# Letting the first chunks enter one a step in a convolution and token-mixing kernel

## The chip, the cores and the metric

The kernel runs on one core of one Trainium2 chip. Times are device microseconds of one execution of the whole program, and lower is better. TensorE (PE in the profile) multiplies, VectorE (DVE) and ScalarE (ACT) work on whole tiles, GpSimd (POOL) and SyncE (SP) mainly issue transfers.

## The reference

The first part is a causal depthwise convolution of seven taps over `x` of shape (8, 4224, 192), with eight heads of 24 channels whose taps are a softmax of `weight`. Its result is the `x` of the second part:

```python
theta = x @ w_theta
cos_t, sin_t = (np.cos(theta), np.sin(theta))
zr = x * cos_t
zi = x * sin_t
yr = np.einsum('ts,bsd->btd', w_tok_r, zr)
yi = np.einsum('ts,bsd->btd', w_tok_i, zi)
y = yr + yi
u = x + y
return (u + np.maximum(u @ w_ch, 0.0)).astype(np.float32)
```

The two token matrices are 4224 x 4224, so nearly all the work is two large matrix products over the tokens, with 8 x 192 = 1536 columns.

## The kernel before, in words

**Chunks and steps.** The 4224 input tokens are cut into 33 chunks of 128 (`NK`), the output tokens into 33 blocks of 128 (`NT`). Output blocks are taken in pairs, 16 pairs and one single block, which makes 17 units (`NU`). A step works on one unit: it multiplies the weights of that unit with every chunk that is active and adds the result to the unit's tile `pv` (128 x 1536 in float32). A chunk is active for 17 steps, so that it meets each unit once. `start[k]` is the step at which chunk `k` becomes active. At most eleven chunks (`NW`) are held at a time, so there are three rounds of eleven; chunk `k + 11` takes the place of chunk `k`. In a step `n` is the number of active chunks.

**Products.** For a pair of blocks the two matrices and two halves (cosine and sine) of a chunk are combined as in a fast 2 x 2 product: 7 products a chunk (a product is one weight tile times 768 columns, two matmuls of 384 columns). The products of a step come in seven runs, one for each combination, each over all `n` chunks; the single block has four runs (five if `n` is at most 2). In the first steps, while `n` is at most `NP`, a pair is multiplied plainly with eight products a chunk (`plain`). A run collects in a PSUM tile `y`, of which there are two buffers, and some runs go on collecting in the tile of an earlier one. After each run `give` adds `y` to a part of `pv` on VectorE (L461), or copies it there on ScalarE in the first round for the parts that are written first (L459).

**What a step needs.** The weights of a step are loaded on POOL's queue into `st` (`load_w`, L374, two steps ahead, one buffer for each of the two matrices), turned by VectorE in 32 x 32 blocks (`turn`, L387) and combined into the sums that the fast product needs (`wsum`, L399), one step ahead. `pv` of the step is loaded from a scratch `part` in device memory (`load_rows`, L425) unless this is the first round, and stored there again after the step (L549), unless it is the unit's last visit. The input `x` of the second part is added to `pv` once for each block: by POOL (`add_x`, L439, `adds`) after a load of the convolution's stored result `xs` into `xr`, or by an adding transfer (`add_ahead`, L448, `ahead`). In the unit's last visit the rest of the reference follows on `pv`: `cast`, a transpose, `output` (L585) and the store of the output.

**What a chunk needs.** A chunk's input `xw` is loaded by POOL's queue (L203) and the overlap with the previous chunk is copied on SP's queue (L194). `xw` and `pv` share six buffers. Its stages are two convolutions on PE (`conv`, L216) with evacuation (L156 or L154) and store to `xs` (L263); twelve transposes (L170) with one evacuation; two `theta` groups on PE (L146), each with two sines on ScalarE (L291); two products on VectorE (`product`, L297); and four differences on VectorE in two calls of `sums` (L306). The tile `z` of a chunk holds all seven operands of the fast product.

**Order.** The order of each engine's work is that in which the program writes it (`pe`, `dve`, `act` and `pool` chain each instruction to the one before); transfers without that wrapper are placed by the framework. Within a step `mix` writes the products and between them the events, which have a position in sevenths of the step. In the second and third round the stages of chunks that start in the next step are events of this step: `places` has two lists of positions, for a first and a second chunk. Chunks are loaded two steps ahead of their start.

In the first round the order is written out by hand at the end of the program: for `i` from 1 to 12, the stages of chunk `i` (convolution, transposes) and of chunk `i - 1` (theta, products, differences) are written with calls of `between` among them, and `between(n)` lets up to `n` products of the stream `flow` pass by `more(n)`, as long as they need no chunk above `ready`. That is at most eleven products for each `i`. After the loop the rest of the stream follows. `NPS` is the last plain step; chunks that started by then get their differences as events of the two steps from `NPS` on.

Of the kernel before, what the change touches and what calls it, by code (L numbers as in the profile page):

```python
# [16 lines left out]
def kernel(  # L17
# [34 lines left out]
    NK = S // P  # L52
# [7 lines left out]
    NU = (NT + 1) // 2  # L60
    NW = 11
    PC = 512
    NP = 4

    base = [0, 0, 1, 1, 2, 3, 3, 4, 4, 5, 5]
    assert len(base) == NW
    start = [base[k % NW] + (NU + 1) * (k // NW) for k in range(NK)]
    NSTEP = start[-1] + NU
    shift = (NU - 1 - (NSTEP - 1)) % NU

# [14 lines left out]
    def pe(ins):  # L85
        return in_order("pe", ins)
# [96 lines left out]
    class Chunk:  # L183


        def __init__(self, k, before=None):
            self.k = k
            self.xw = wk.tile([2 * WR, 2, B, D], F16, name="xw", tag="big", bufs=6)
            for a in range(NQ):
                h, lo = a // 2, (a % 2) * WR  # L190
                t0 = token(k, a)
                hist = self.xw[lo : lo + HALO, h, :, :]
                if before is not None:
                    nc.sync.dma_start(  # L194
                        out=hist, in_=before.xw[lo + Q : lo + Q + HALO, h, :, :]
                    )
                elif t0 == 0:
                    nc.vector.memset(hist, 0.0)
                else:
                    lo, t0 = lo - HALO, t0 - HALO  # L200
                lo += HALO
                n = (a % 2 + 1) * WR - lo
                nc.gpsimd.dma_start(  # L203
                    out=self.xw[lo : lo + n, h, :, :],
                    in_=x[:, t0 : t0 + n, :].rearrange("b s d -> s b d"),
                )
# [117 lines left out]
    def load_chunk(k):  # L324
        if k < NK and k not in chunks:
            chunks[k] = Chunk(k, before=chunks[k - 1] if k % NW else None)

    def active(t):
        return [k for k in range(NK) if start[k] <= t < start[k] + NU]

    def unit(t):
        return (t + shift) % NU

    class Step:


        def __init__(self, t):
            self.t, self.u, self.ks = t, unit(t), active(t)
            self.n = len(self.ks)
            self.tbs = [tb for tb in (2 * self.u, 2 * self.u + 1) if tb < NT]  # L340
            self.pair = len(self.tbs) == 2
            self.first = t < NU
            self.final = t + NU >= NSTEP
            self.late = self.final and self.n < NW
            visits = [v for v in range(NU, NSTEP) if v % NU == t % NU]
            quiet = [v for v in visits if start[2 * NW - 1] < v <= 2 * NU]
            self.adds, self.ahead = [], []
            for i, tb in enumerate(self.tbs):
                known = self.known(tb)
                if t not in ([v for v in quiet if known < v - 1] or visits[-1:])[:1]:  # L350
                    continue
                if not self.late:
                    self.adds.append(i)
                else:
                    far = known <= start[2 * NW - 1]
                    self.ahead.append((i, 2 * NU - NW + 2 * (t % NU) if far else start[-1],
                                       (t // NU - 1 - far) % 2))
            self.plain = self.first and self.pair and self.n <= NP
            self.time = 0.324 * self.n * (8 if self.plain else 7 if self.pair else 5 if self.n <= 2 else 4)
            self.closing = False  # L360
            self.st, self.w, self.xr, self.ub, self.uT, self.pv = {}, {}, {}, {}, {}, []
# [274 lines left out]
    steps = [Step(t) for t in range(NSTEP)]  # L636
# [75 lines left out]
    for a in range(2):  # L712
        nc.gpsimd.affine_select(
            out=sel, in_=sel, pattern=[[1, Q - 1 + 2 * WR]], channel_multiplier=-1,
            base=-(Q - 1 + HALO - KS + 1 + a * WR), compare_op=ALU.not_equal, fill=1.0,
# [13 lines left out]
    def idle(n):  # L729
        for _ in range(n):  # L730
            pe(nc.tensor.matmul(
                spare[:, 0, 0:BH], lhsT=noise[:, 0:P], rhs=noise, start=True, stop=True
            ))
# [30 lines left out]
    for q in range(Q):  # L764
# [3 lines left out]
            start=True, stop=True,  # L768
# [16 lines left out]
    flow = stream()  # L785
    need = [None]

    def more(n):

        for i in range(n):  # L790
            if need[0] is None:
                need[0] = next(flow, NK)
            if need[0] > ready[0]:
                return n - i
            need[0] = next(flow, NK)
        return 0

    steps[0].load_rows()
# [4 lines left out]
    for m in (1, 2):  # L803
        steps[1].load_w(m)
    load_chunk(4)
    load_chunk(5)
    for g in range(NG):
        chunks[0].conv_batches(g)
    idle(2)
# [2 lines left out]
    for i in range(1, NW + 2):  # L812
        ch = chunks.get(i) if i < NW else None
        old = chunks[i - 1] if i <= NW else None

        def between(n):
            left = more(n)
            if i < 3:
                idle(min(left, 2) if i == 1 else 0)

        if ch:
            ch.conv(0)
        between(2)
        if old:
            old.theta(0)
        ready[0] = i - 2
        between(1)
        if ch:
            ch.conv(1)
        between(2)  # L830
        if old:
            old.theta(1)
        if i in (1, 3):
            for name in ("11", "21"):
                steps[i // 2].turn(name)
        if i + 3 < NW:
            load_chunk(i + 3)
        between(1)
        if i == 1:
            for first in (Z11, Z21):  # L840
                old.product(first, slice(0, 1))
        if ch:
            ch.transpose()
        if i == 1:
            for first in (Z11, Z21):
                old.product(first, slice(1, 2))
        elif old:
            old.product(Z11)
        between(2)
        if i > 1 and old:  # L850
            old.product(Z21)
        if i in (1, 3):
            for name in ("12", "22"):
                steps[i // 2].turn(name)
        between(1)
        if old and start[i - 1] > NPS:
            old.sums(0)
        between(1)
        if old and start[i - 1] > NPS:
            old.sums(1)  # L860
        between(1)
    ready[0] = NK
    for _ in flow:
        pass
# [31 lines left out]
```

## Time and profile before

| | |
|---|---|
| median of three runs | 1437.17 us (1435.09 to 1443.39) |
| the profiled execution, its own time | 1437.8 us |
| its span, first to last instruction | 1436.0 us |
| granted TensorE clock, mean | 0.999 |
| products: `y` matmuls at L536 | 7672, 1282.4 us busy |
| VectorE additions at L461 | 317, mean 954 ns |
| weight turns at L387, 11 chunks wide | 140, mean 1635 ns |
| weight sums at L399, 11 chunks wide | 136, mean 905 ns |
| loads and stores of `pv` | 79 each of 768 KB |
| POOL additions at L439 | 24, mean 3103 ns |
| bytes read and written in device memory | 245.49 MB and 108.13 MB |

PE, PEld, DVE, ACT and POOL are the engines, PEld being the loading of weights into TensorE. A stretch of the profile shows for each engine the busy time in it. The time of one instruction overlaps a little with the next one's on VectorE and ScalarE, so that the distance from start to start is some 0.06 to 0.1 us shorter than the duration. Busy times of matmuls are modelled; the distance of their starts is exact. The DMA share is the sum of all packets' times over 16 engines, and can be above 1 since an engine works on packets of several queues.

### The profile page before, as it was taken

The page shows a single profiled execution, that of the slowest core. Times are in us where ns is not written, and L with a number is a line of the kernel's source. Part 1 is how long each engine was busy: PE and PEld are TensorE (multiplying, and loading weights), DVE is VectorE, ACT ScalarE, POOL GpSimd, SP SyncE. Part 2 cuts the span into 40 slices and gives each one's busy share as a digit, 9 for nine tenths or more (in the row PEclk, how much of TensorE's full clock was granted, in tenths as well). Part 3 has the DMA queues.
Part 4 walks back from the last instruction along what each step waited for, and adds up shares of the span by engine and source line. Part 5 has one row for each costly group of instructions (what it writes and reads, how often), then busy time and mean ns, then how long its engine had stood idle before and what let it go on. Part 6 is the DMA issues. An engine that isn't in the chain of part 4 may idle for free.

```text
span 1436.0 us, 23771 instructions
## 1 busy us (share of the span) xinstructions
PE 1409.4 (98%) x9829; PEld 889.7 (62%) x9829; DVE 973.0 (68%) x1046; ACT 310.6 (22%) x374; POOL 434.3 (30%) x655
## 2 busy tenths in 40 slices
PE   8889999999999999999999999999999999999997
PEld 5556666666666666666666666666566666666665
DVE  6893554545548787866665657877777677767676
ACT  5851101111124244000000004335100110010133
POOL 8511211111233332532333343233323123213110
PEclk9999999999999999999999999999999999999999
DMA  9975766564799999898899889999999999999894
GB/s 193 234 164 132 147 125 128 100 151 89 147 232 227 231 236 239 209 256 177 232 236 229 229 157 243 231 198 255 248 206 216 215 206 220 203 202 197 166 214 136
DMA packets 272045, 281.99 MB, mean 196 GB/s; under 512 B 106688, under 2 KB 240192, under 8 KB 271936
## 3 DMA queue, kind: packets, MB, share of 16 engines
q0 software_dynamic: 162464, 92.15, 48.8%
q1 hardware_dynamic: 71840, 178.88, 35.4%
q10 hardware_dynamic: 37632, 9.44, 4.5%
q8 instruction: 77, 1.26, 0.4%
q14 instruction: 32, 0.26, 0.1%
HBM read 245.49 MB, written 108.13 MB: 246 GB/s over the span
## 4 chain that ended last, share of the span: by engine, by line
PE 92%; DMA 2%; DVE 2%; ACT 1%; SPq 1%; issue 1%; POOL 0%; DVEq 0%; ACTq 0%; POOLq 0%
PE y L536 84%; PE v L146 5%; PE tp L170 1%; PE pc L216 1%; ACT z L291 1%; DMA xw<-in_x_dram 1%; DMA xw<-xw 1%; SPq L194 1%; DVE pv L461 0%; DVE z L306 0%; DVE pv L585 0%; DMA part<-pv 0%; DMA st<-in_moe_w_tok_r_dram 0%; DMA wsb<-in_weight_dram 0%; DVE wt L399 0%
## 5 line engine op out<-in xcount | busy, mean ns | idle before, releaser
L536 PE MATMUL y<-z,wt 128*128 128x384 f16 x7672 | 1282.4, 326 | 6.4 <-DVE pv L461 5.3
L536 PEld LDWEIGHTS <-wt 128*128 128x128 f16 x7672 | 743.7, 98 | 482.6 <-issue 6.3
L461 DVE TENSOR_TENSOR pv<-y,pv 128x768 f32<-128x768 f32 x317 | 302.5, 954 | 323.9 <-PE y L536 284.0
L387 DVE STREAM_TRANSPOSE wt<-st 128x1408 f16<-128x1408 f16 (+7 forms) x224 | 327.5, 1465 | 51.0 <-PE y L536 38.3
L374 POOL DMA_DIRECT2D st<-in_moe_w_tok_r_dram x232 | 132.3, 578 | 463.5 <-DVE wt L387 451.8
L374 POOL DMA_DIRECT2D st<-in_moe_w_tok_i_dram x232 | 132.4, 579 | 405.0 <-DVE wt L387 396.5
L399 DVE TENSOR_TENSOR wt<-wt 128x1408 f16<-128x1408 f16 (+6 forms) x208 | 173.4, 834 | 40.5 <-PE y L536 38.3
L156 ACT ACTIVATE z<-pc 128x768 f16<-128x768 f32 (+1 forms) x62 | 47.5, 803 | 387.0 <-PE pc L216 378.4
L156 ACT ACTIVATE ub<-pv 128x768 f16<-128x768 f32 x63 | 50.2, 836 | 343.6 <-DVE pv L461 315.9
L459 ACT ACTIVATE pv<-y 128x768 f32<-128x768 f32 x66 | 53.7, 814 | 280.5 <-PE y L536 280.5
L146 PEld LDWEIGHTS <-uT 128*128 128x128 f16 x1056 | 90.6, 98 | 23.8 <-issue 5.9
L439 POOL TENSOR_TENSOR pv<-pv,xr 128x1536 f32<-128x1536 f32 x24 | 74.5, 3103 | 66.2 <-issue 26.7
L203 POOL DMA_DIRECT2D xw<-in_x_dram x132 | 76.3, 587 | 27.1 <-issue 7.0
L585 DVE SCALAR_TENSOR_TENSOR pv<-v,pv 128x768 f32<-128x768 f32 (+1 forms) x67 | 62.8, 942 | 24.9 <-PE v L146 24.5
L306 DVE TENSOR_TENSOR z<-z 128x768 f16<-128x768 f16 x132 | 71.2, 552 | 2.2
L291 ACT ACTIVATE z<-v,half_pi 128x768 f16<-128x768 f32 x66 | 59.6, 903 | 56.4 <-PE v L146 55.7
L156 ACT ACTIVATE uT<-tp 128x1536 f16<-128x1536 f16 (+1 forms) x47 | 56.5, 1208 | 47.3 <-PE tp L170 47.3
L297 DVE TENSOR_TENSOR z<-z 128x1536 f16<-128x1536 f16 (+1 forms) x68 | 60.6, 926 | 4.3 <-ACT z L291 4.2
L146 PE MATMUL v<-wth,uT 128*128 128x192 f16 x528 | 54.4, 246 | 2.7 <-ACT z L291 2.1
L146 PE MATMUL v<-wch,uT 128*128 128x192 f16 x528 | 54.3, 246 | 1.3 <-DVE pv L585 0.7
L291 ACT ACTIVATE z<-v 128x768 f16<-128x768 f32 x66 | 53.2, 806 | 0.0
L216 PE MATMUL pc<-xw,bands 96*64 96x192 f16 x512 | 30.4, 251 | 5.4 <-DMA st<-in_moe_w_tok_r_dram 2.7
(45 smaller groups left out, 144.8 us busy)
## 6 DMA issues: line engine op xcount, KB each, us to landing
part<-pv SPq DMA_DIRECT2D x79, 768.0 KB, 4.3
pv<-part SPq DMA_DIRECT2D x79, 768.0 KB, 6.0
out_dram<-pv SPq DMA_DIRECT2D x65, 384.0 KB, 4.5
st<-in_moe_w_tok_r_dram POOLq DMA_DIRECT2D x136, 176.0 KB, 6.0
st<-in_moe_w_tok_i_dram POOLq DMA_DIRECT2D x136, 176.0 KB, 5.3
xs<-z SPq DMA_DIRECT2D x132, 96.0 KB, 5.1
xw<-in_x_dram POOLq DMA_DIRECT2D x121, 96.0 KB, 6.2
xr<-xs SPq DMA_DIRECT2D x24, 384.0 KB, 4.5
```

The lines of the kernel that those rows point to most:

```text
L146: pe(nc.tensor.matmul(v[:, k, b * D : (b + 1) * D], lhsT=tT[:, 3 * k + b + i, :], rhs=w[:, 2 * b + i, :], start=(i == 0), stop=(i == 1),))
L156: act(nc.scalar.activation(out=out, in_=in_, func=AT.Copy))
L203: nc.gpsimd.dma_start(out=self.xw[lo : lo + n, h, :, :], in_=x[:, t0 : t0 + n, :].rearrange("b s d -> s b d"),)
L291: act(nc.scalar.activation(**args))
L306: dve(nc.vector.tensor_tensor(out=z[:, o, :], in0=z[:, a, :], in1=z[:, b, :], op=ALU.subtract))
L374: pool(nc.gpsimd.dma_start(out=st[a * Q : (a + 1) * Q, 0:nb, :, 0:n] .rearrange("i r bt s -> i (r bt) s"), in_=w[self.tbs[0] * P : (self.t ...
L387: dve(nc.vector.transpose(self.w[name][:, 0 : self.n, :, :], self.st[int(name[1])][:, int(name[0]) - 1, :, 0 : self.n * Q] .rearrange("p b ...
L399: dve(nc.vector.tensor_tensor(out=self.w[name][:, 0 : self.n, :, :], in0=self.w[a][:, 0 : self.n, :, :], in1=self.w[b][:, 0 : self.n, :, : ...
L439: ins = pool(nc.gpsimd.tensor_tensor(out=self.pv[i], in0=self.pv[i], in1=self.xr[i], op=ALU.add))
L461: dve(nc.vector.tensor_tensor(out=o, in0=yv, in1=o, op=ALU.add))
L536: pe(nc.tensor.matmul(y[cn][:, q, 0:BH], lhsT=self.w[wn][:, c, :, :].rearrange("p bt i -> p (bt i)"), rhs=chunks[k].z[:, zn, q * BH : (q + ...
L585: dve(nc.vector.scalar_tensor_tensor(out=ub[:, ks, :], in0=v[:, ks, :], scalar=0.0, in1=ub[:, ks, :], op0=ALU.max, op1=ALU.add,))
```

## The change

The chunks of the first round start one a step over steps 0 to 9 (the first two together), where they started two a step or one over steps 0 to 5. The second round starts over steps 20 to 27 for 18 to 23, the third over 40 to 45 for 36 to 41. The program has 62 steps for 58. The assertion says that a chunk's predecessor has left when it starts.

`NP` is 3 for 4, so that the plain steps are those with two and three chunks. In the hand-written part `between` gets a position on a scale of 13, and lets products pass up to that share of the products that have become possible with the chunk before last; chunk 5 is loaded in the loop and not ahead of it, and each later one two turns of the loop ahead for three. The blocks whose `x` is added early are chosen from a wider range of steps (`quiet`), and the step of an adding transfer is worked out in another way.

```diff
-    NP = 4
-
-    base = [0, 0, 1, 1, 2, 3, 3, 4, 4, 5, 5]
-    assert len(base) == NW
-    start = [base[k % NW] + (NU + 1) * (k // NW) for k in range(NK)]
+    NP = 3
+
+    bases = ([0, 0, 1, 2, 3, 4, 5, 6, 7, 8, 9],
+             [2, 2, 3, 4, 4, 5, 6, 6, 7, 8, 9],
+             [4, 4, 5, 5, 6, 7, 7, 8, 8, 9, 9])
+    start = [b + (NU + 1) * r for r, base in enumerate(bases) for b in base]
+    assert len(start) == NK and all(
+        start[k + NW] > start[k] + NU for k in range(NK - NW)
+    )
...
-            quiet = [v for v in visits if start[2 * NW - 1] < v <= 2 * NU]
+            quiet = [v for v in visits if start[2 * NW - 1] - 5 < v <= 2 * NU]
...
-                    self.ahead.append((i, 2 * NU - NW + 2 * (t % NU) if far else start[-1],
+                    self.ahead.append((i, start[2 * NW - 1] + 2 * (t - NSTEP + 6) if far else start[-1],
                                        (t // NU - 1 - far) % 2))
...
+    done = [0]
+    chunk_of = [s.ks[item[3]] for s in steps for item in s.products()]
+
+    def reach(r):
+
+        return next((i for i, k in enumerate(chunk_of) if k > r), len(chunk_of))
+
     def more(n):
...
             need[0] = next(flow, NK)
+            done[0] += 1
         return 0
...
-    load_chunk(5)
...
-        def between(n):
-            left = more(n)
-            if i < 3:
-                idle(min(left, 2) if i == 1 else 0)
+        lo, hi = reach(i - 3), reach(i - 2)
+
+        def between(n, upto):
+            left = more(max(0, round(lo + (hi - lo) * upto / 13) - done[0]))
+            if i == 1:
+                idle(min(n, 2))
...
-        between(2)
+        between(2, 0)
...
-        between(1)
+        between(1, 1)
...
-        between(2)
+        between(2, 3)
...
-        if i + 3 < NW:
-            load_chunk(i + 3)
-        between(1)
+        if i > 2:
+            load_chunk(min(i + 2, NW - 1))
+        between(1, 4.5)
...
-        between(2)
+        between(2, 6.5)
...
-        between(1)
+        between(1, 8)
...
-        between(1)
+        between(1, 9.5)
...
-        between(1)
+        between(1, 11)
```

## The prediction

> **What bounds the kernel now.** I read the page first, then the busy time by stretch with a stretch for each step, then VectorE's timeline inside one step, then the POOL additions. The page says that TensorE is the bound almost everywhere:
>
> ```profile
> PE 1409.4 (98%) x9829; PEld 889.7 (62%) x9829; DVE 973.0 (68%) x1046; ACT 310.6 (22%) x374; POOL 434.3 (30%) x655
> ...
> PE 92%; DMA 2%; DVE 2%; ACT 1%; SPq 1%; issue 1%; POOL 0%; DVEq 0%; ACTq 0%; POOLq 0%
> ```
>
> So time can only come from places where PE is not back to back. I found each step's ends by counting the `y` matmuls. The columns are width, then busy time (and count) of PE, PEld, DVE, ACT, POOL, then the granted clock, the DMA share and GB/s. The rows are steps 0, 1, 2, 3 (the run-in), 5, 36 and 40:
>
> ```profile
> 20.89:34.63 13.74, 12.66 (x131) 8.48 (x129) 10.28 (x14) 11.06 (x15) 10.53 (x19) 1.00 1.32 234
> 34.63:58.28 23.65, 20.25 (x191) 13.37 (x189) 16.68 (x28) 20.11 (x26) 13.35 (x24) 1.00 1.29 224
> 58.28:84.02 25.74, 22.17 (x213) 14.48 (x212) 25.38 (x40) 21.38 (x27) 8.08 (x15) 1.00 1.11 230
> 84.02:105.23 21.21, 19.08 (x135) 12.07 (x134) 19.43 (x25) 10.23 (x13) 4.55 (x8) 1.00 0.63 144
> ...
> 125.71:150.73 25.02, 25.02 (x155) 15.06 (x154) 6.84 (x6) 3.24 (x4) 4.57 (x8) 1.00 0.62 131
> ...
> 887.86:914.09 26.23, 26.23 (x216) 17.42 (x214) 22.45 (x28) 12.32 (x14) 6.87 (x12) 1.00 1.06 255
> ...
> 992.44:1010.34 17.90, 17.63 (x162) 12.05 (x160) 16.45 (x19) 11.99 (x14) 3.77 (x7) 1.00 1.05 325
> ```
>
> Step 5 does 77 products (7 of each of 11 chunks) in 25.02 us: 0.325 us a product. Step 36 does 63 products and prepares two chunks in 26.23: (26.23 - 63 x 0.325) / 2 = 2.88 us of PE for one chunk's stages. By these two figures steps 0 to 3 have 132 products (42.9 us) and some nine chunks' stages (26.1), 69.0 in all, and take 84.3: **15.4 us lost in the run-in** (2.4, 5.1, 5.3, 2.6 by step). Nothing is lost in steps 4 to 37. Steps 38 to 41 lose 3.8 (3.1 of it in step 41), the last four 4.8. The chance to gain is the 15.4; the rest is a chance to lose.
>
> **Why the entry steps stand on an edge.** Step 36, VectorE, from the fourth run's addition to the sixth's:
>
> ```profile
> 904.20 0.96 DVE L461 TENSOR_TENSOR pv<-y,pv 128x768 f32<-128x768 f32 x1
> 905.07 2.20 DVE L306 TENSOR_TENSOR z<-z 128x768 f16<-128x768 f16 x4
> 907.19 1.50 DVE L387 STREAM_TRANSPOSE wt<-st 128x1280 f16<-128x1280 f16 x1
> 908.62 0.92 DVE L461 TENSOR_TENSOR pv<-y,pv 128x768 f32<-128x768 f32 x1
> 909.46 0.81 DVE L399 TENSOR_TENSOR wt<-wt 128x1280 f16<-128x1280 f16 x1
> 910.18 1.82 DVE L297 TENSOR_TENSOR z<-z 128x1536 f16<-128x1536 f16 x2
> 911.92 1.14 DVE L306 TENSOR_TENSOR z<-z 128x768 f16<-128x768 f16 x2
> 912.98 0.95 DVE L461 TENSOR_TENSOR pv<-y,pv 128x768 f32<-128x768 f32 x1
> ```
>
> There is no gap in it: 904.20 to 913.93, 9.73 us. With two `y` buffers the next step's first run may not open before that last addition has ended; PE reached it at 914.09, 0.16 us later. VectorE's chain does not get shorter with fewer chunks except in its one transpose and one weight difference (1.43 and 0.72 us from start to start at ten chunks, 1.30 and 0.66 at nine), while PE's three runs shrink by 0.975 us for each chunk less.
>
> **The change, part by part.** From the start lists, the third round's entry steps have 6, 7, 7, 7, 8, 9 chunks (steps 39 to 44) for 9, 9, 10, 9, 9, 9 (35 to 40); the second's are 7, 8, 8, 9, 9, 10, 10, 10 (19 to 26) for 9, 9, 10, 9, 9, 9.
>
> *Products.* Two plain steps with 2 and 3 chunks for 2 and 4: 3835 products for 3836, **-0.3**. No matmul is added by the four more steps.
>
> *Run-in.* Products between two arrivals are now 20, 19, 29, 36, 43, 50, 57, 64: with 2.88 each, PE periods of 9.4, 9.1, 12.3, 14.6 us and longer. In one period ACT has four sines (3.4), two evacuations (1.6), one transpose evacuation (1.5) and four copies of `y` (3.3): 9.8, so it ties in the first two and is free later. VectorE has two products and four differences (4.1), three additions (2.9) and the next weights (3.9 at four chunks): 10.9, and 4.8 of differences for the plain steps' three chunks once. That ties until chunk 5 too. Step 0's 2.4 stays, since nothing ahead of it changes. I put 2 on the ties and 3 on `y` copies that queue behind sines in runs of 1.3 to 2 us. So 7.4 of 15.4 remain: **-8.0** (ends -4.5 and -12). Loading chunk 5 later and the stores of `pv` earlier lie within periods longer than the loads' median 6.2 us.
>
> *Four more steps.* 28 more additions of 0.954 (26.7 us of VectorE), 8 more stores and 8 more loads of `pv`, 32 more weight loads of 0.58 us on POOL's queue and 16 more stores and loads on SP's. Steps without chunk stages hide it: VectorE is busy 6.84 to 20 of 25 us there. That cover is missing where chunks enter:
>
> *Chain against runs.* PE has three runs (0.975 n), two theta groups (1.31) and 0.2 less for the start; VectorE 7.57 and the transpose and difference of the next step (1.56 at seven chunks, 1.75 at eight, 1.96 at nine). Step 19 (7, next 8): 7.94 against 9.32, 1.4 short. Step 21 (8, next 9): 8.91 against 9.53, 0.6. Step 39 (6, next 7): 6.96 against 9.13, 2.2. Step 40 (7, 7): 1.2. Step 42 (7, 8): 1.4. Step 43, before a single block, has no difference: 0. With one chunk the check is two runs against an addition, four differences, a transpose, an addition: steps 20 and 41 are 0.1 and 0.6 short. That is 7.5; the run before the chain is also 0.3 to 0.6 too short in each of these, so about 1.7 more: **+9.2** (ends 4, where differences overlap better, and 13).
>
> *POOL's additions.* Four additions of `x` move into steps 22 to 24, three of them beside a chunk's 16-bit operations (at 3.6 and 5.6 sevenths). Such a pair in the trace:
>
> ```profile
> 604.48 3.10 POOL L439 TENSOR_TENSOR pv<-pv,xr 128x1536 f32<-128x1536 f32 x1 [9.02 <-issue]
> 605.31 3.02 DVE L399 TENSOR_TENSOR wt<-wt 128x1408 f16<-128x1408 f16 x1
> ```
>
> The difference took 3.02 for a median 0.88: it ended 0.75 after POOL did. Three times 2.1, less slacks of 0.2 to 0.9: **+4.5** (0, if they fall into gaps, to 9). The eight in steps 52 to 55 stand beside no chunk stage, as those of steps 42 to 51 do today without loss: 0.
>
> *Transfers.* A `pv` tile is 128 packets of 6144 B at 234 ns over 16 engines, 1.87 us; a pair's weights are 2048 packets; a chunk some 5.0 in all. Steps 38 to 44 then want 158 us of DMA in 141 us of step, a share of 1.12, where steps 35 to 40 ran at 1.01 and the first two steps at 1.3. The landing records put the second chunk of a step close: chunk 25 landed 1.5 us ahead of its convolution, 14 0.4, 28 0.2 behind it. Shorter steps take about 1.9 off such leads: **+2** (0 to 6).
>
> The weights' rows fall from 576 B and more to 384 and 448 B there. Packets of 704, 576, 448 and 384 B took 73, 64, 54 and 49 ns: no step between 576 and 448. The Trainium skill's page "DMA: Bandwidth & Descriptors", section Specifications, gives 512 B as the least transfer for full rate and has shorter ones read, modify and write, which speaks against this change. If that doubled the packets of 448 B and less, steps 38 to 41 would ask for some 27 us more and the change would end near 1470; the rows show no such thing, so I give it nothing.
>
> Sum: -0.3 - 8.0 + 9.2 + 4.5 + 2 = **+7.4** on the profiled 1437.8 us (its span 1436.0): 1445.2. The median of the runs shown is 1437.2, so 1444.6.
>
> **The rivals.**
> *The other side: the run-in is cured whole.* If ACT and VectorE really keep up from chunk 3 on, 13.0 goes (all but step 0's 2.4); with the chain's lower end (4) and the two small terms at 0, 1437.2 - 0.3 - 13 + 4 = 1428. For it: ACT is busy 20.1 and 21.4 us in steps 1 and 2, and each period is longer than its 9.8. Against: VectorE at 25.38 of 25.74 in step 2. It decides while all that the later rounds pay stays under 6.1.
> *POOL and transfers cost nothing:* -0.3 - 8 + 9.2 = +0.9, 1438.
> *DMA becomes the bound in the third entry.* If 1.01 is all that this mix gets, 158 us of transfers take 157 for 141: 15.6, of which 8.5 is counted, 1452. Against: 1.3 in steps 0 and 1.
> *The run-in is not helped:* chunks are paced by the first loads and by VectorE whatever the order; the 8.0 is gone, 1452.6.
>
> **How the numbers follow.** 0.5% (7.2 us) is about what a measurement of this kernel can tell from no change. My sum has 0.45, spread over both sides of 1444.4 (0.20 within, 0.25 above; its own range 1438 to 1451); the whole cure 0.20 (0.16 under 1430, 0.04 within); no cost of POOL and transfers 0.12; DMA bound 0.15; no help 0.08. That is faster 0.16, same 0.36, slower 0.48. With the ends of the terms, 1431 to 1456 leaves out 0.2.
>
> **What would show it.** Right: steps 1 to 3 back to back from about 45 us; in steps 19, 39, 40 and 42 PE idle before a `y` matmul at a step's start, released by VectorE's addition at L461; 3 us differences at L306 or products at L297 beside L439 in steps 23 and 24. Wrong: no PE idle in steps 17 to 26, or convolutions that wait for `xw` by more than 3 us each from step 39 on, or a run-in that still loses over 11 us.

## The result, and the profile after

The changed kernel takes **1498.55 us** (median of four runs, 1495.09 to 1503.51) beside 1436.72 for the kernel before on the same chip: a ratio of 1.0424, 95% interval 1.0379 to 1.0468. The forecast was 1444.6, with 1431 to 1456 as its range. The direction was the likelier one; the size was missed by 54 us. The profiled execution took 1497.8 us (span 1496.1), and its lines are those of `after`: line numbers behind the start lists are four higher than before (L540 for the `y` matmuls at L536, L465 for the additions at L461, L443 for POOL's additions, L207 for the loads of `x`, L220 for the convolution).

The page of the changed kernel, engine times and the chain that ended last:

```profile
PE 1424.9 (95%) x9827; PEld 894.6 (60%) x9827; DVE 1008.1 (67%) x1106; ACT 309.5 (21%) x374; POOL 461.0 (31%) x683
...
PE 80%; DMA 9%; DVE 6%; POOL 2%; issue 2%; ACT 1%; SPq 1%; DVEq 0%; POOLq 0%; ACTq 0%
```

PE has two matmuls fewer and is busy 15.5 us longer, and the share of DMA in the chain rose from 2% to 9%. So something besides idle time grew, and transfers are now the largest part of the chain beside PE's own work. Busy time by stretch, one stretch for each of steps 0, 1, 2, 3, 19, 23, 39 and 41 (same columns as in the prediction; the last three are granted clock, DMA share, GB/s):

```profile
20.33:31.94 11.61, 10.10 (x98) 7.00 (x97) 7.11 (x10) 8.88 (x12) 8.53 (x16) 1.00 1.25 208
31.94:45.63 13.69, 11.79 (x103) 7.28 (x100) 7.30 (x14) 9.21 (x12) 8.46 (x15) 1.00 1.32 261
45.63:65.82 20.19, 14.30 (x102) 8.36 (x101) 18.96 (x33) 9.67 (x13) 9.18 (x16) 0.92 1.17 219
65.82:81.87 16.05, 14.92 (x115) 9.18 (x115) 11.95 (x18) 8.44 (x11) 6.84 (x12) 1.00 1.03 213
...
415.63:449.08 33.45, 24.69 (x188) 15.93 (x186) 20.11 (x26) 12.00 (x14) 8.84 (x16) 0.85 1.02 220
...
522.59:563.14 40.55, 28.88 (x216) 18.47 (x214) 27.37 (x26) 12.33 (x14) 17.48 (x16) 0.90 0.84 199
...
923.15:955.37 32.22, 23.47 (x174) 14.94 (x172) 19.35 (x26) 12.04 (x14) 9.51 (x17) 0.89 0.97 210
...
978.52:1005.67 27.15, 21.80 (x142) 13.33 (x142) 17.42 (x23) 6.06 (x7) 9.18 (x16) 0.87 0.96 205
```

Steps 19 and 39 need 21.7 and 19.4 us by the prediction's figures (49 and 42 products, two chunks at 2.88) and take 33.45 and 32.22. The granted clock, 1.00 in every entry step of before, is 0.85 to 0.90 in the four entry steps shown.

I took each step's matmuls, subtracted from the distances of their starts what the same sequence takes undisturbed, and put each excess down to the matmul that came late. An entry is the stretch of steps in which the chunks of the second or the third round are prepared and become active. In us of PE, before and after:

| | before | after | difference | forecast |
|---|---|---|---|---|
| run-in, all causes | 15.4 | 17.0 | +1.6 | -8.0 |
| entries: a convolution late | 0.2 | 29.4 | +29.2 | +2 (transfers) |
| entries: slower matmuls (clock) | 0.2 | 11.8 | +11.6 | not counted |
| entries: first run of steps 19 to 21 and 39 to 42 late | 0 | 11.7 | +11.7 | +9.2 (chain) |
| entries: `y` late in steps 23 and 24 | 0 | 8.2 | +8.2 | +4.5 (POOL) |
| entries: `y` late in the last entry step (41, now 45) | 3.1 | 2.9 | -0.2 | 0 |
| last steps | 4.6 | 4.6 | 0 | 0 |

With 0.3 for one product less that makes 62 us. The medians are 61.8 apart; the spans of the two profiles, from which the table is made, 60.1, of which the time ahead of the first `y` matmul (20.33 us for 20.89) and the last step (14.54 for 15.24) explain 1.3 of the 1.7 us between.

**The late convolutions.** PE's timeline at the start of step 19:

```profile
418.11 0.24 PE L220 MATMUL pc<-xw,bands 96*64 96x192 f16 x1 [1.99 <-DMA xw<-in_x_dram]
423.51 1.49 PE L220 MATMUL pc<-xw,bands 96*64 96x192 f16 x15 [5.17 <-DMA xw<-in_x_dram]
424.93 4.35 PE L540 MATMUL y<-z,wt 128*128 128x384 f16 x14
429.12 0.83 PE L174 MATMUL tp<-ident,z 128*128 128x128 f16 x12
429.79 2.44 PE L540 MATMUL y<-z,wt 128*128 128x384 f16 x14
```

The convolution of chunk 11 waits twice for its own input. The lines after it show the second cost: 14 matmuls take 4.35 us right behind the gap and 2.44 five us later. And this is POOL's queue ahead of it:

```profile
402.50 2.29 POOL L378 DMA_DIRECT2D st<-in_moe_w_tok_r_dram  x4 [8.95 <-DVE wt L391]
404.78 0.63 POOL L207 DMA_DIRECT2D xw<-in_x_dram  x1
410.30 2.29 POOL L378 DMA_DIRECT2D st<-in_moe_w_tok_i_dram  x4 [4.89 <-DVE wt L391]
412.57 1.87 POOL L207 DMA_DIRECT2D xw<-in_x_dram  x3
415.34 2.28 POOL L207 DMA_DIRECT2D xw<-in_x_dram  x4 [0.90 <-issue]
```

One of the four loads of chunk 11 goes out at 404.8. The other three stand behind the second weight load, which waits until VectorE has turned the weights that lie in its buffer (4.89 us of idle time, released by L391). They go out from 412.6 on and the last lands at 423.5; PE wanted them at 416.1. The same place in the kernel before (step 16, 390.3 to 415.3 us; the second four loads are chunk 12's):

```profile
394.40 2.47 POOL L203 DMA_DIRECT2D xw<-in_x_dram  x4
401.91 1.18 POOL L203 DMA_DIRECT2D xw<-in_x_dram  x2 [5.04 <-issue]
403.65 1.22 POOL L203 DMA_DIRECT2D xw<-in_x_dram  x2 [0.56 <-DMA st<-in_moe_w_tok_r_dram]
407.35 2.28 POOL L374 DMA_DIRECT2D st<-in_moe_w_tok_i_dram  x4 [2.48 <-DVE wt L387]
```

There all eight loads go out ahead of the second weight load, chunk 11's first 21.3 us ahead of its convolution. The program writes a chunk's load at 4.5 sevenths of a step and the second weight load at 4.3, but only the weight loads are chained to the order of POOL's work; the loads of `x` are placed by the framework, in some steps ahead of that weight load and in others behind it. Behind it, what is left until a first convolution at 0.1 of the next step is 2.6 sevenths at most: 9.3 us in a step of 25.0 (step 16 of before), 6.8 in one of 18.2 (step 18 of after).

Chunk 11 had 9.0 us to spare before. Now its last load lands 5.4 us behind its first matmul, which was itself 2.0 late; chunks 15, 18, 22, 23 and 26 are 3.4, 6.2, 2.4, 4.3 and 4.2 late. Each of these six has at least one load behind the second weight load of its step, though the last wait of chunk 23 (4.13 us) is for its overlap copy, which SP's queue issued at 932.11 behind two loads of `pv`. No chunk whose loads all go out ahead of that weight load is late by them. Before, 23 of the 88 loads of the two later rounds stand behind it, all of a step's second chunk, whose convolution comes two sevenths later; after, 32 do, and chunks 11, 22 and 26 are first chunks. Why the framework placed them otherwise is not shown.

**The additions on POOL.** Timeline of VectorE and POOL in step 23:

```profile
545.96 4.72 DVE L301 TENSOR_TENSOR z<-z 128x1536 f16<-128x1536 f16 x2
546.17 3.69 POOL L443 TENSOR_TENSOR pv<-pv,xr 128x1536 f32<-128x1536 f32 x1 [13.31 <-DVE wt L403]
...
558.31 3.91 DVE L310 TENSOR_TENSOR z<-z 128x768 f16<-128x768 f16 x2
558.48 3.33 POOL L443 TENSOR_TENSOR pv<-pv,xr 128x1536 f32<-128x1536 f32 x1 [0.81 <-DVE z L301]
```

Two products take 4.72 us for 1.82, two differences 3.91 for 1.14: what was forecast, and larger, since both ran into the full length of an addition.

### The profile page after: what moved, and what is told of

Its sections match the earlier page's. It is cut to its first block, busy times and chain, and to the rows that moved or that the text cites. A ratio compares the mean times of both kernels' runs of the same rounds, so it can differ in the third digit from the quotient of the medians.

```text
span 1496.1 us, 23946 instructions
## 1 busy us (share of the span) xinstructions
PE 1424.9 (95%) x9827; PEld 894.6 (60%) x9827; DVE 1008.1 (67%) x1106; ACT 309.5 (21%) x374; POOL 461.0 (31%) x683
## 4 chain that ended last, share of the span: by engine, by line
PE 80%; DMA 9%; DVE 6%; POOL 2%; issue 2%; ACT 1%; SPq 1%; DVEq 0%; POOLq 0%; ACTq 0%
PE y L540 73%; PE v L150 4%; DMA xw<-in_x_dram 4%; DVE pv L465 2%; DMA xw<-xw 2%; POOL st L378 1%; PE pc L220 1%; DVE z L301 1%; DMA part<-pv 1%; PE tp L174 1%; DVE wt L391 1%; DVE z L310 1%; DVE wt L403 1%; DMA xs<-z 1%; DMA st<-in_moe_w_tok_r_dram 1%
## 5 line engine op out<-in xcount | busy, mean ns | idle before, releaser
L540 PE MATMUL y<-z,wt 128*128 128x384 f16 x7670 | 1296.0, 328 | 30.8 <-DVE pv L465 24.1
L540 PEld LDWEIGHTS <-wt 128*128 128x128 f16 x7670 | 746.6, 98 | 518.1 <-issue 45.2
L465 DVE TENSOR_TENSOR pv<-y,pv 128x768 f32<-128x768 f32 x345 | 329.2, 954 | 355.8 <-PE y L540 299.6
L391 DVE STREAM_TRANSPOSE wt<-st 128x1408 f16<-128x1408 f16 (+9 forms) x240 | 329.4, 1378 | 45.5 <-PE y L540 33.8
L378 POOL DMA_DIRECT2D st<-in_moe_w_tok_r_dram x248 | 142.0, 581 | 458.1 <-DVE wt L391 450.3
L378 POOL DMA_DIRECT2D st<-in_moe_w_tok_i_dram x248 | 141.9, 581 | 398.3 <-DVE wt L391 395.8
L403 DVE TENSOR_TENSOR wt<-wt 128x1408 f16<-128x1408 f16 (+7 forms) x224 | 175.0, 781 | 41.4 <-PE y L540 39.0
L443 POOL TENSOR_TENSOR pv<-pv,xr 128x1536 f32<-128x1536 f32 x28 | 88.4, 3156 | 87.3 <-DVE pv L589 38.4
L207 POOL DMA_DIRECT2D xw<-in_x_dram x132 | 76.8, 592 | 52.4 <-DMA part<-pv 20.5
L310 DVE TENSOR_TENSOR z<-z 128x768 f16<-128x768 f16 x132 | 74.5, 574 | 2.2
L301 DVE TENSOR_TENSOR z<-z 128x1536 f16<-128x1536 f16 (+1 forms) x68 | 66.4, 1008 | 2.5 <-ACT z L295 2.5
L220 PE MATMUL pc<-xw,bands 96*64 96x192 f16 x512 | 34.3, 267 | 27.8 <-DMA xw<-in_x_dram 22.4
```

The source lines that it names most:

```text
L207: nc.gpsimd.dma_start(out=self.xw[lo : lo + n, h, :, :], in_=x[:, t0 : t0 + n, :].rearrange("b s d -> s b d"),)
L301: dve(nc.vector.tensor_tensor(out=o, in0=xv, in1=o, op=ALU.mult))
L310: dve(nc.vector.tensor_tensor(out=z[:, o, :], in0=z[:, a, :], in1=z[:, b, :], op=ALU.subtract))
L378: pool(nc.gpsimd.dma_start(out=st[a * Q : (a + 1) * Q, 0:nb, :, 0:n] .rearrange("i r bt s -> i (r bt) s"), in_=w[self.tbs[0] * P : (self.t ...
L391: dve(nc.vector.transpose(self.w[name][:, 0 : self.n, :, :], self.st[int(name[1])][:, int(name[0]) - 1, :, 0 : self.n * Q] .rearrange("p b ...
L403: dve(nc.vector.tensor_tensor(out=self.w[name][:, 0 : self.n, :, :], in0=self.w[a][:, 0 : self.n, :, :], in1=self.w[b][:, 0 : self.n, :, : ...
```

## The experiments

**1. Where the time of the entries goes.** Four kernels were run beside each other. The first takes the new range of `quiet` back:

```diff
-            quiet = [v for v in visits if start[2 * NW - 1] - 5 < v <= 2 * NU]
+            quiet = [v for v in visits if start[2 * NW - 1] < v <= 2 * NU]
```

> The changed kernel without the wider choice of blocks (no - 5 in quiet): the four POOL additions of steps 22 to 24 become adding transfers at steps 29 and 31. Theory 1 (POOL's additions block VectorE's 16-bit operations and nothing else): the waits of y matmuls in steps 23 and 24 (8.2 us in the changed kernel) fall under 1, and 2 to 3 of slow clock go with them, the convolution waits of step 23 (6.9) stay: 1487 to 1490 for 1498.5. Theory 2 (the additions also hold the x loads behind them in POOL's queue): the convolution waits of step 23 fall too, 1478 to 1483. Rival (the additions cost nothing): within 3 us of the changed kernel.

1491.13 us (ratio 1.0368, 1.0327 to 1.0408). The late `y` of steps 23 and 24 goes from 8.2 us to 0.2, so POOL's additions made it, where they fall in this kernel: in the next one, `early`, the same four additions are still there, beside other work of VectorE, and `y` matmuls of steps 23 to 25 wait 2.1 us. The late convolutions of step 23 stay (7.0 us), and those of the third entry grow from 11.3 to 19.6: what was gained was partly lost again to the same late loads.

The second asks for the chunks earlier in their step, and changes nothing else:

```diff
-                found.append((4.5, lambda k=k: load_chunk(k)))
+                found.append((1.25, lambda k=k: load_chunk(k)))
```

> The changed kernel with a chunk's load written at 1.25 sevenths of the step instead of 4.5, two steps ahead of its start as before. Theory 1 (the x loads are late because they are written behind the second weight load, which waits for VectorE): convolution waits fall from 29 us (steps 19 to 24: 18, 39 to 43: 11) to under 8 and the slow clock with them, 1460 to 1473. Rival 1 (buffers: the six shared by xw and pv come free only when a pv store has landed, so an earlier place does not issue earlier): waits of 20 us or more stay, 1488 to 1500. Rival 2 (transfers themselves are the bound in these steps): x lands earlier but weights or pv land later, and y matmuls or weight turns wait instead, 1490 to 1505.

1458.24 us (1.0154, 1.0124 to 1.0185): **40 us of the 62**, by the late convolutions, the clock behind them and some 6 us of the late `y`, less what other waits took up. Steps 19 and 23 in busy time by stretch:

```profile
419.49:442.94 23.45, 21.85 (x189) 14.68 (x187) 20.11 (x26) 11.99 (x14) 9.11 (x16) 1.00 1.15 262
...
513.00:540.75 27.75, 26.39 (x215) 17.41 (x214) 23.40 (x26) 12.33 (x14) 14.73 (x18) 1.00 1.05 251
```

Step 19 is 10.0 us shorter, of which 2.84 is PE busy for less time, with the clock at 1.00 again. No convolution of the entries waits; the loads land 9.3 us and more ahead. The DMA share went up, from 1.02 to 1.15, so it was not the transfers' rate that held step 19.

The third has longer entries with a larger `n` in them (and the old `quiet`):

```diff
-             [2, 2, 3, 4, 4, 5, 6, 6, 7, 8, 9],
-             [4, 4, 5, 5, 6, 7, 7, 8, 8, 9, 9])
+             [0, 0, 1, 2, 3, 4, 5, 6, 7, 8, 9],
+             [1, 1, 2, 3, 4, 5, 6, 7, 8, 9, 9])
```

> Second and third round entering one chunk a step (second over steps 18 to 27, third over 37 to 45, the last two together), first round as in the changed kernel, without the - 5; still 62 steps, and the last steps have 9, 8, 7, 6, 5, 4, 3, 2 chunks. Theory (the loss is where an entry step has under nine chunks and two chunks' stages): steps 17 to 45 lose under 6 us for 64 in the changed kernel; the longer leave costs some 5 to 10 at the end; 1438 to 1452. Rival (four more steps with their stores, loads and additions are what costs, wherever they lie): 1480 or more.

1459.58 us (1.0162, 1.0139 to 1.0185), above the 1438 to 1452 expected. The second entry, one chunk a step with nine or more active, loses 0.1 us, the third 10.0 (7.1 of it in one late step). So the second entry's loss is not one of a longer entry as such. Whether few active chunks or two arrivals a step make it, this kernel does not separate, since it changes both. The rest of this kernel's 23 us lies in its longer leave (the last steps lose 7.5 for 4.6, and late steps have transposes of their own on PE), which I did not take apart.

The fourth has the start lists, `NP` and `quiet` of before, and only the new hand-written loop:

> The kernel before (its start lists, four plain chunks, 58 steps) with only the new written-out loop: products let through by the share of those that have become possible, chunk 5 loaded in the loop. Theory (the run-in is bound by late weights and VectorE, not by where products stand among a chunk's stages): steps 0 to 5 lose 13 to 19 us where the kernel before loses 15.4, 1434 to 1441. Rival (the even spread itself helps the run-in): 1428 to 1433. Rival (the new loop holds products back, since chunks enter two a step): 1445 or more.

1445.03 us (1.0053, 1.0035 to 1.0070), 21.0 lost in the run-in. The new loop is no help to the old start list.

**2. The place in the queue, or the time?** `early` moves the loads past both weight loads. This one moves them only across the second, from 4.5 to 4.25 (the second weight load stands at 4.3):

```diff
-                found.append((4.5, lambda k=k: load_chunk(k)))
+                found.append((4.25, lambda k=k: load_chunk(k)))
```

> The changed kernel with a chunk's load written at 4.25 sevenths for 4.5, so only from just behind the second weight load (4.3) to just ahead of it in POOL's queue; the PE, VectorE and ScalarE programs are the same. Theory (a load behind the weight load waits with it for VectorE's transpose at 4.2, and lands too late for convolutions at 0.1 of the next step): convolution waits fall from 29 us to under 8, 1458 to 1470. Rival (it is lead time as such, that is the 3.25 sevenths that the early run gave): a quarter of a seventh is 0.7 us, so waits of over 20 us stay, 1488 to 1500. Rival (buffers): the same, 1488 to 1500.

1469.01 us (1.0227, 1.0193 to 1.0261), 29.5 less than after. The instructions of PE, VectorE and ScalarE are the same and in the same order. POOL's queue at the place shown above:

```profile
403.82 2.29 POOL L378 DMA_DIRECT2D st<-in_moe_w_tok_r_dram  x4 [8.96 <-DVE wt L391]
406.10 3.62 POOL L207 DMA_DIRECT2D xw<-in_x_dram  x6
...
413.25 2.29 POOL L378 DMA_DIRECT2D st<-in_moe_w_tok_i_dram  x4 [1.85 <-DVE pv L465]
```

The seven loads that stood behind the weight load go out ahead of it, 7 to 8 us sooner in their step; chunk 11 lands 3.7 us early, and PE's waits for convolutions are gone in the second and the third round, with margins of 0.2 to 10 us. Only chunks 15 and 30 still have loads behind that weight load. A quarter of a seventh of a step, some 0.7 us, decides 30 us, because it decides what the loads queue behind: the steps are as short as in the changed kernel. The 10.8 us from here to `early` are not convolutions, which wait in neither. Steps 21 to 24 lose 12.0 us here and 2.4 there, most of it before `y` matmuls: 7.2 us in steps 23 and 24, beside POOL's additions.

**3. VectorE's chain.** From here on the kernels have `early` and the old `quiet`. First with step 1's turns of weights moved ahead in the run-in:

```diff
-            for name in ("11", "21"):
+            for name in ("11", "21") if i == 1 else ("12", "22"):
...
-        if i in (1, 3):
-            for name in ("12", "22"):
-                steps[i // 2].turn(name)
+        if i in (1, 2):
+            for name in ("12", "22") if i == 1 else ("11", "21"):
+                steps[i - 1].turn(name)
```

> The changed kernel with the early load place (1.25 sevenths) and without the - 5, and with step 1's four weight turns one place earlier in the written-out loop (11 and 21 in turn 2, 12 and 22 in the first place of turn 3), so that the weights of step 2 can be loaded some 4 us earlier. Theory for the run-in (VectorE stands idle 4.3 us at 39.4 for step 2's weights and then runs behind): the run-in loses 10 to 14 us for 19.3 in the early run; with the POOL additions gone as well 1446 to 1453. Rival (VectorE's own work bounds steps 1 and 2): 18 or more, 1453 to 1458.

1453.5 us (1.0123, 1.0106 to 1.0140). The second entry loses 3.5 us, the third 15.6, the run-in 16.4 for 19.3 in `early`, where 10 to 14 had been expected. Then, without that move, the last four stages of a step's second chunk are put later, all behind the addition of the sixth run:

```diff
-                (2.1, 2.1, 3.55, 4.6, 5.0, 5.5, 5.55, 5.8, 6.0),
+                (2.1, 2.1, 3.55, 4.6, 5.0, 6.02, 6.05, 6.4, 6.6),
```

> The changed kernel with the early load place and without the - 5, and with the second chunk's two products and four differences moved behind the sixth run's addition (positions 6.02 to 6.6 for 5.5 to 6.0), run-in as in the changed kernel. Theory (the wait of y matmuls at the start of a step after two chunks is the chain up to the sixth run's addition): the waits of steps 19, 21, 40 and 42 (1.8, 0.8, 1.5 to 3.5, 1.8 us in the early run) fall under 0.5 each, and up to 1 us may come back at the next step's second addition; 2nd and 3rd entry lose under 14 us for 25.6. Rival (VectorE has too much work in these steps whatever its order): the same waits one run later, within 2 us.

1448.2 us (1.0081, 1.0068 to 1.0094). The late first runs of steps 19, 21 and 42 are gone, as they must be if it is VectorE's chain ahead of the step's last addition that makes them. Steps 39, 40 and 41, with six and seven chunks, keep 2.3, 2.6 and 3.6: PE now waits for an addition before the last run of the step (910.10, 934.06) and early in the next one (916.22, 940.18), so the moved stages hold other additions.

**4. The same edits on the kernel before.** Turns alone, loads alone, loads and positions:

> The kernel before with step 1's four weight turns one place earlier in the written-out loop, nothing else. Theory (late weights of step 2 hold the run-in, VectorE idle 5.0 us at 34): the run-in loses 11 to 13.5 us for 15.4, 1433 to 1435, a little faster than before. Rival (ACT and the x loads bound it there): within 1 us of 1436.6, or a loss where VectorE waits for weights that have not landed.

> The kernel before with a chunk's load written at 1.25 sevenths for 4.5. Theory (in steps of 26 us the later place is in time; landing margins are 5 to 18 us except three under 2): only the 0.2 us of convolution wait goes, within 2 us of 1436.6. Rival (the late place costs the kernel before too, through transfers that pile up in steps 39 to 41): step 41's 3.1 us shrink, 1432 to 1434.

> The kernel before with both repairs: load place 1.25 and the second chunk's last stages behind the sixth addition. Theory: its entry steps have 0.16 us of slack, so the chain costs nothing to move, step 41 loses 1 us for 3.1, 1433.5 to 1436. Rival: the moved stages delay the next step's second addition by 1 to 2 us in the steps with two chunks, 1438 to 1444.

1437.45 (1.0005, 0.9996 to 1.0013), 1435.70 (0.9992, 0.9983 to 1.0001) and **1435.22 (0.9982, 0.9970 to 0.9993)**. The last is the one kernel here whose interval lies below before, by 0.2%; step 41's stall is 1.5 us there for 3.1. The turns alone were expected to help the run-in, and it loses 17.2 us for 15.4. Before had nothing to win from earlier loads in its entries, since its margins there were 0.4 to 18 us but for one of -0.2.

**5. The run-in.** In `chain` steps 0 to 4 lose 2.2, 2.6, 8.9, 1.8 and 1.7 us. Six kernels ask why step 2 does. One profile tells only so much here: the program of the run-in is the same in `after`, `early`, `p425`, `quiet`, `ones` and `chain`, whose run-ins lose 17.0, 19.3, 18.2, 18.6, 17.3 and 17.7 us, in step 2 alone 8.2 to 10.5. First `chain` without the load of chunk 5, whose convolution reads chunk 4's rows again:

```diff
+            if k == 5:
+                self.xw = before.xw
+                return
```

> The chain kernel (early load place, no - 5, second chunk's last stages behind the sixth addition) with chunk 5's load and overlap copies left out: it convolves chunk 4's rows again, so that its output differs for that chunk. Theory (in the run-in the transfers are full, share 1.3, and step 2's second weights land 4.1 us after VectorE could turn them): they land 2 to 5 us earlier, VectorE's wait of 4.3 us goes, and steps 1 to 4 lose 8 to 11 us for 15.0. Rival (VectorE and ScalarE have too much work there): 14 or more.

`chain` with the hand-written loop of before, of which this is the core:

```diff
-            left = more(max(0, round(lo + (hi - lo) * upto / 13) - done[0]))
+            left = more(n)
```

> The chain kernel with the written-out loop of the kernel before (up to eleven products after each chunk, chunks 4 and 5 loaded ahead) and the new start lists. Theory (the run-in is held by work of ScalarE and VectorE and by transfers that any order has to fit in): steps 0 to 10 lose 13 to 18 us for 17.8, 1445 to 1449 in all. Rival (the spread loop is what worsens the run-in, as with 1445.0 for 1436.6 in the spread run): 9 to 12 us, 1440 to 1443.

1447.97 (1.0073, 1.0045 to 1.0100) and 1447.17 (1.0061, 1.0039 to 1.0083); run-ins of 17.0 and 19.0. Neither one load nor the order of the products is it. In the first, VectorE got its second weights in time for step 2 and then idled 3.54 us at 57.6 for those of step 3; PE's gap from 56 to 60 us took the clock down to 0.50 until 65, so the loss stayed at 8.2.

Then VectorE's work, the buffer of the weights, and both. `nosums` leaves out the twelve differences of the plain steps' chunks (their products read the cosine half of `z` in place of them); `st3` gives the second weights of steps 2 to 4 buffers that nothing else uses in the first round:

```diff
+            if m == 2 and 2 <= self.t <= 4:
+                one = self.t == 4
+                st = wk.tile([P, N], F16, name="st", tag="xr" if one else "ub",
+                             bufs=1 if one else 2)
...
-                        rhs=chunks[k].z[:, zn, q * BH : (q + 1) * BH],
+                        rhs=chunks[k].z[:, Z11 if start[k] <= NPS and zn in (T1, T2, T3, T4) else zn, q * BH : (q + 1) * BH],
...
-        if t in (NPS, NPS + 1):
+        if False and t in (NPS, NPS + 1):
```

> The kernel chain without the twelve differences of VectorE that the chunks of the plain steps get in steps 1 and 2; the products of these three chunks read the cosine half of z in place of the differences, so the products, their count and their order stay. In chain steps 0 to 4 lose 2.2, 2.6, 8.9, 1.8, 1.7 us of PE, 17.8 in the run-in, median 1448.2. Theory 1 (VectorE has too much work in steps 1 and 2): some 12 x 0.52 = 6 us leave its chain, step 2 loses 3 to 4 and the kernel ends near 1443. Theory 2 (the second weights of step 2 come late, VectorE idles for them from about 41 to 45.7 us): the idle time grows by what is left out, step 2 still loses 7 or more, and the kernel ends at 1446.5 to 1448.5.

> The kernel chain with the second weights of steps 2, 3 and 4 loaded into buffers that nothing else uses in the first round, so that their loads no longer wait for VectorE's turn of the step before. Theory 2 (late second weights): they land some 4 to 8 us sooner, VectorE's 4.75 us of idle time ahead of 45.69 goes, step 2 loses 4 to 5 us and the kernel ends near 1444. Theory 1 (VectorE's work) or a limit of the transfers themselves, which have a share of 1.3 there: the loss stays within 1.5 us of chain's, 1447 to 1449.

> Both edits on chain: the second weights of steps 2 to 4 in buffers of their own, and the twelve differences of the plain steps' chunks left out (those chunks' products read the cosine half of z in their place). If the two causes stand one behind the other, neither alone frees step 2 and both do: step 2 loses 2 to 3 us and the kernel ends near 1441. If one of them is all, this ends within 1 us of that one. If the transfers limit it, step 2 still loses over 6 and the kernel ends above 1446.

1447.41 (1.0077, 1.0062 to 1.0092), 1446.46 (1.0073, 1.0058 to 1.0088) and 1445.08 us (1.0062, 1.0045 to 1.0079). Step 2 loses 7.1, 7.7 and 6.9 us for 8.9, not far below what it loses in kernels with the same run-in. Both theories fall as whole causes: what is taken out of VectorE's work comes back as idle time ahead of the same turn (6.80 us for 4.75), and with a free buffer VectorE has the second weights only 1.9 us sooner (1.3 counted from the first `y` matmul). VectorE and PE of the kernel with both edits, end of step 2 (the turn, sum and addition are L397, L409 and L471 here, the `y` matmul L546):

```profile
52.09 0.49 DVE L409 TENSOR_TENSOR wt<-wt 128x640 f16<-128x640 f16 x1
52.73 2.44 PE L546 MATMUL y<-z,wt 128*128 128x384 f16 x14
55.62 0.85 DVE L397 STREAM_TRANSPOSE wt<-st 128x640 f16<-128x640 f16 x1 [3.03 <-DMA st<-in_moe_w_tok_i_dram]
...
58.25 0.95 DVE L471 TENSOR_TENSOR pv<-y,pv 128x768 f32<-128x768 f32 x1
...
59.26 0.99 PE L546 MATMUL y<-z,wt 128*128 128x384 f16 x5 [4.09 <-DVE pv L471]
```

PE stops at 55.17 with both `y` buffers full. The addition that would free one stands in VectorE's queue behind the turn of step 3's second weights, and that waits for a load. POOL issued it from 45.63 to 49.35, with a share of DMA of 1.38 and 1.34 in the ten-us stretches from 40 and from 50 us in the kernel with the free buffer alone. So the additions of an early step wait for weights of the next one. That the loads are slow because the transfers are full fits these shares; that fewer bytes would cure it is not shown. Last, the same buffers in the best kernel so far:

> The kernel before with the x loads at 1.25 and the second chunk's later positions (the run early_chain_before, 1435.2), and the second weights of steps 1 and 2 in buffers of their own. Before loses 15.4 us in its run-in with VectorE idle 4.97 us ahead of 39.02 for weights. If late weights hold that run-in too, it loses 3 to 5 us less and ends near 1431; if the chunks themselves set the pace, within 1.5 us of 1435.

1436.69 us (0.9997, 0.9987 to 1.0006): no gain, a run-in of 16.1.

## Why the prediction was wrong

**Transfers, +2 (0 to 6): the step that failed, by 27 us and 11.6 more of clock.** I asked whether the transfers have room (a share of 1.12) and how close the landings were, and took 1.9 us off the leads because steps get shorter. I did not follow POOL's queue, and took the loads to keep their places in it. They did not: ahead of the two entries all 16 loads went out before the second weight load in the kernel before (steps 16 and 34), and in the changed one (steps 18 and 38) 13 of 16 went out behind it, so that they waited for VectorE's turn, in steps of 18.2 us for 25.0. The late convolutions cost 29.2 us more. `p425` puts the loads ahead of the weight load in steps as short, and no convolution of the entries waits; a shorter lead alone, which is what the 1.9 us stood for, stays within my 0 to 6 there. The sign that I had named for being wrong came: convolutions that wait by more than 3 us.

**The clock was no term at all.** Before has a granted clock of 1.00 in all entry steps, so no row of it showed a price. A convolution that is 5 us late also slows the 4 to 6 us of matmuls behind it (the clock of 0.50 in the rows further down).

**Run-in, -8.0: wrong, +1.6** (2 to 4 in the profiles of the other kernels with the same run-in). Waits for convolutions and `theta` did shrink, from 6.1 and 3.4 us to 0.5 and 0.8, as meant. But 12.6 us of waits for `y` took their place (3.5 before). I had compared work with period for each engine, and VectorE's tie was counted as work (10.9); what the rows above show is its order, additions behind turns that wait for loads. No kernel here took that wait away, so how much of the 12.6 us it makes stays open. Another sign I had named came, a run-in that loses over 11. The rival that had this, "not helped", got 0.08; the loads' median of 6.2 us, which I set against the periods, says nothing of when a load is issued.

**VectorE's chain, +9.2 (4 to 13): right**, 11.7 measured, and in the steps named: 2.0, 0.8 and 0.8 us in steps 19 to 21 (forecast 1.4, 0.1 and 0.6, before the run ahead of the chain), and 3.0, 1.5, 1.8 and 1.8 in 39 to 42 (2.2, 1.2, 0.6, 1.4). `chain` took three of them away.

**POOL's additions, +4.5 (0 to 9): the mechanism right, the size near its end**, 8.2, taken away by `quiet`. The 2.1 us of `early` and the 7.2 of `p425`, with the same additions, show that the size hangs on what they fall beside, which is in part luck.

**DMA as the bound, given 0.15: not what happened.** `early` ran step 39 at a share of 1.06 with no convolution late, and step 19 at 1.15. Nor did the 384 and 448 B rows of steps 38 to 41 cost what the prediction's estimate from 512 B would give: it ended near 1470, and `chain` ends at 1448.2 with the same rows. In its trace, as in that of the changed kernel, packets of 576, 512, 448 and 384 B on POOL's queue took a median of 65, 60, 55 and 51 ns: no step at 512.

What is left of `chain` over before, 12.7 us by span (1448.7 for 1436.0), is 9.5 in the third entry, 2.4 in the run-in and 1.0 in the second entry.

## What to carry to other kernels

A load that no order binds can change its place in the issuing queue when a change moves the work around it, and a lead that is given in shares of a step shrinks with the step. When a change makes steps shorter, list for each load its place in the issuing queue, what stands ahead of it and what that waits for, before any sum of bytes. An engine that works in order can hold finished work (here an addition that frees a PSUM buffer) behind an early preparation whose data has not landed; equal work and period then say nothing. And a stall of TensorE of 5 us cost more than 5 here, so it has to be priced at more.

## What the runs showed of the hardware

The granted clock in stretches of 2 us around the gap of step 19 of the changed kernel:

```profile
420.00:422.00 2.00, 0.00 (x0) 0.00 (x0) 0.00 (x0) 0.00 (x0) 0.00 (x0) 0.50 1.28 293
...
426.00:428.00 2.00, 2.00 (x8) 0.93 (x7) 0.00 (x0) 0.00 (x0) 0.00 (x0) 0.50 0.98 372
```

PE stops at 416.1 but for one short matmul; the clock is 0.65 in the stretch from 418, 0.50 from 420 to 428, 0.79 in the next and 1.00 from 430, so it came back some 5 us after work did at 423.5. In step 23 a gap of 5.96 us gave a like course. The Trainium skill, "TensorE: Matmul & The Clock Gate", Part 1, has the clock halved after an idle window of about 3.4 us and restored after about as long of sustained work. These rows agree in kind: the clock fell some 2.5 us after the stop and came back some 5 us after the start. The length of a gap alone does not settle it here: the wait of 2.17 us in step 39 took the clock to 0.50 in the stretch from 928 to 930, the wait of 3.19 us at 481.58 in step 21 left it at 1.00. The gap of step 19 cost 2.8 us on top of the wait.

Of the two products beside POOL's addition the first took 0.95 us, the second 3.85, and it ended 0.8 us after the addition, about one product's own time: so the second hardly advanced until POOL was done. The skill's page "SBUF — State Buffer", section "SBUF: two separate sides", says that the port pair that both engines share is held for a whole instruction and the other engine blocks; the row agrees.

A DMA share above 1 does not take several queues: in the trace of the kernel before, queue 0 alone had up to 39 packets under way at a time, over 16 engines.
